# Two encoder layers on one core: the second layer's rows 1024 to 1535 in halves, the order of the residual work, and a windowed rule for repeated score matmuls

## The chip, the cores and the metric

The kernel runs on one core of a Trainium2 chip (trn2). The metric is the device time of one execution in microseconds, the median of several runs. Only bf16 inputs and a bf16 output of 2048 x 512 cross the memory; everything else stays on the core.

## What is computed

Two identical layers, each an attention block with a residual, then a dense block with a residual:

```python
# x: 1 x 2048 x 512, H = 32 heads of Dh = 16, Dff = 1792
def _A_ref(x, wqkv, wo):
    q, k, v = ...                       # (x @ wqkv) split into 3 x 32 heads of 16
    scores = jnp.einsum("bhqd,bhkd->bhqk", q, k) * (Dh ** -0.5)
    p = _softmax(scores, axis=-1)
    o = jnp.einsum("bhqk,bhkd->bhqd", p, v)
    return (o to B, S, D) @ wo

def _B_ref(x, w1, w2):
    h = jnp.maximum(x @ w1, 0)
    return h @ w2

x = x + _A_ref(_layernorm(x), A_wqkv, A_wo)
x = x + _B_ref(_layernorm(x), B_w1, B_w2)
x = x + _A_ref(_layernorm(x), A_wqkv, A_wo)
x = x + _B_ref(_layernorm(x), B_w1, B_w2)
```

Each layer has 32 x 2048 x 2048 exponentials, and both products around them have only 16 as one of their sizes.

## The kernel before

The program is one long unrolled stream, ordered by a list scheduler that runs while the program is built. It keeps a model of the time on TensorE (PE) and VectorE (DVE), in nanoseconds, and decides from it what is issued next.

The stream is cut into **slots**. A slot makes three blocks of scores (each 128 keys x 512 queries of one head, four heads side by side in the 32-row groups of the array), into three banks of PSUM; ScalarE (ACT) takes their exponential in one instruction. In some slots the third block goes to VectorE instead, which computes the exponential of two such blocks (a **pair**) with a polynomial in six kinds of step (`lin`, `step`, `cube`). PV products of earlier slots, and **residual work**, fill TensorE between the score triples. Residual work of a chunk of rows is: the output projection (o), the second layernorm with its transposes, the first dense product with relu (h), the second dense product (z), and in layer one also the next layernorm, k and v. It waits in the queue `work`.

The rows of a layer are worked through in chunks; `TPC` is 4 tiles of 128 rows. Layer two's last 512 rows are already cut in two:

```python
    chunks = {(l, j): (j * TPC, TPC) for l in range(2) for j in range(NQS)}   # NQS = 4
    chunks[1, NQS - 1] = (NKB - TPC, TPC // 2)
    chunks[1, NQS] = (NKB - TPC // 2, TPC // 2)
```

When the last head of a chunk has ended, its residual work goes behind all that still waits:

```python
    def before(l, j):          # whose buffers this chunk overwrites
        if (l, j) == (0, 0):
            return None
        return (l, min(j, NQS - 1) - 1) if j else (0, NQS - 1)

    def rest_of_chunk(l, j):
        b = before(l, j)
        xj, a, w = columns(l, j)
        n = w // P
        war_h = each(chunks[b][1], "z", *b) if b else []
        war_x = each(NF, "h", *b) if b else []
        gs = [o_group(l, j, i) for i in range(n)]
        gs += ln_groups(("ln2", l, j), xn2T, a, n, war_x)
        gs += [h_group(l, j, ft, war_h) for ft in range(0, NF, QS // w)]
        if (l, j) != (1, NQS - 1):
            gs += [z_group(l, j, i) for i in range(n)]
        ...                                        # layer one: ln1, k, v of the next layer
        return gs
    ...
        if ended[l, j] == NT and not last:
            work.extend(rest_of_chunk(l, j))
```

How much residual work a slot gets is paced so that it ends about with the next chunk, and it is only issued where the model leaves room before the next scores are needed:

```python
        pace = ( ... max(todo / max(rest + (0.0 if first["j"] == NQS - 1 and not first["l"] else AHEAD[first["l"]] if first["j"] < NQS - 1 else -6.0), 6.0), 0.5) )
        owed[0] = min(owed[0] + pace, 6.0) if todo else 0.0
        ...
        need_by = exp_end[no - 1] - MM - PE_TO_ACT
        limit = max(need_by - 60.0, s_ready) - SWITCH
```

A slot may write its three score blocks more than once, with the same values, to keep TensorE streaming; how often is found from the work of this slot alone and a small carry `level`:

```python
        spare = int(max(need_by - pe_start("s", s_ready), 0.0) / MM)       # MM = 216
        soon = (len(pend) > 1) + (owed[0] > 1.0 and (bool(cur) or not evac))
        short = FLOOR * 1330.0 - level - busy[0] - MM * (1 + soon)         # FLOOR = 0.56
        times = 1 + min(spare, max(0, math.ceil(short / MM)))
        ...
        for _ in range(times):
            pe_run("s", 1, s_ready)
            for a, (sg, kb, g) in sorted(zip(place, now), key=in_turn):
                nc.tensor.matmul(b[:, a : a + sg["w"]], kt[...], qbuf[...], start=True, stop=True,
                                 tile_position=(32 * g, 0))
        ...
        ex = nc.scalar.activation(out=eb[:, 0 : place[m]], in_=b[:, 0 : place[m]], func=ACTF.Exp, ...)   # L1249
```

After the last slot comes a tail that is written out by hand: what is left in the queue (`run_all`), then o, layernorm, h and z of the last 256 rows, and between them the z of the 256 rows before, whose two tiles of 128 rows are `half_part(0, ...)` (during the layernorm) and `half_part(1, ...)` (one matmul after each step of h):

```python
    run_all()
    l, j = 1, NQS
    ...                                     # o of the last rows, x, layernorm
    half_part(0, range(NF))
    ...                                     # transposes
    for ft in range(NF + 1):
        if ft < NF:
            ...                             # 4 matmuls of h (256 wide), relu on ACT or DVE in turn, load of w1
        if ft:
            for i in rows:
                add(banks[i], ht[ft - 1][:, part(i)], w2[:, ft - 1, :], False, ft == NF, "h")
        if ft < NF:
            half_part(1, [ft])
```

Of the kernel before, what the change touches and what calls it, by code (L numbers as in the profile page):

```python
# [24 lines left out]
def kernel(  # L25
# [20 lines left out]
    NF = DFF // P  # L46
    NTT = S // P
    NKB = S // P
    NDC = D // P
    QS = 512  # L50
    NQS = S // QS
    TPC = QS // P
# [20 lines left out]
    MM = 216.0  # L73
# [7 lines left out]
    AHEAD = (8.0, 8.0)  # L81
# [8 lines left out]
    LATE = 0.0  # L90
    BACKLOG = 6000.0
    HASTE = 12
    FULL = 3

    ctx.enter_context(tc.manual_schedule())
# [129 lines left out]

    slot = [0]
    now_pe = [0.0]
    now_dve = [0.0]  # L230
    mode = [None]
# [21 lines left out]
    def pe_start(kind, ready=0.0):  # L253
        return max(now_pe[0] + (SWITCH if mode[0] != kind else 0.0), ready)

    def pe_run(kind, units, ready=0.0):
        now_pe[0] = pe_start(kind, ready) + units * MM
        mode[0] = kind
        busy[0] += units * MM

# [7 lines left out]
    work = []  # L268
# [169 lines left out]


    chunks = {(l, j): (j * TPC, TPC) for l in range(2) for j in range(NQS)}  # L440
    chunks[1, NQS - 1] = (NKB - TPC, TPC // 2)
    chunks[1, NQS] = (NKB - TPC // 2, TPC // 2)

    def columns(l, j):

# [72 lines left out]
    def ln_rows(tag, tt, n, i):  # L518

        if tag not in ln_seq:  # L520
            ln_seq.append(tag)
        at_tag = ln_seq.index(tag)
        prev = ln_seq[at_tag - 1]
        old = [("xn", ln_seq[at_tag - 2], k) for k in range(TPC)] if at_tag > 1 else []
        if ("st", tag, i) not in made:
            task(830, lambda: ln_stats(tag, tt + i, i), [("st", tag, i)], old)
        if i == n - 1:

            def rstd():
                ln_rstd(tag, 0)  # L530
                ln_newton(tag)
                mark(("rs", tag, 3), lag=RSTD_LAG)

            task(500, rstd, [("rs", tag, 3)], each(n, "st", tag) + old)
            for k in range(n):
                task(
                    325, lambda k=k: ln_apply(tag, tt + k, k), [("xn", tag, k)],
                    [("xT", prev, k), ("rs", tag, 3)],
                )

    def ln_groups(tag, dst, at_column, n, war):
        groups = []
        for i in range(n):

            def piece(i=i):
                pt = ln_transpose(tag, i)

                def fin():
                    a = at_column + i * P
                    nc.vector.tensor_copy(out=dst[:, :, a : a + P], in_=pt)  # L550
                    mark(("xnT", tag, i))

                put_evac(342, fin)

            groups.append(
                group([(1.3, piece)], [("xT", tag, i), ("xnT", tag, i)], [("xn", tag, i)] + war)
            )
        return groups

    def each(n, *key):  # L560
        return [key + (i,) for i in range(n)]
# [63 lines left out]
    def o_group(l, j, i):  # L625
        tt, n = chunks[l, j]
        a = columns(l, j)[1] + i * P

        def fin(b):
            nc.vector.tensor_add(out=x_t[tt + i][:], in0=x_t[tt + i][:], in1=b)  # L630
            mark(("o", l, j, i))
            ln_rows(("ln2", l, j), tt, n, i)

        return mm_group(
            [(ot[t][:, a : a + P], wo[:, t // 2, :]) for t in range(NT)], fin,
            [("o", l, j, i)],
            [("ot", l, j, t, i) for t in range(NT)],
        )
# [11 lines left out]
    def h_group(l, j, ft, war):  # L650
        n = (l * NQS + j) * NF + ft
        _, a, w = columns(l, j)

        number = QS // w
        fts = range(ft, ft + number)
        made_here = [("h", l, j, f) for f in fts]

        def fin(b):
            out = htp[ft // 2][:, ft % 2 : ft % 2 + number, a : a + w]
            sums = b.rearrange("p (f q) -> p f q", f=number)  # L660
            if ending[0]:
                nc.scalar.activation(out=out, in_=sums, func=ACTF.Relu)
            else:
                nc.vector.tensor_scalar(  # L664
                    out=out, in0=sums, scalar1=0.0, scalar2=None, op0=ALU.max
                )
            for key in made_here:
                mark(key)

        def after():  # L670
            for f in range(number):
                load_w1(n + f + NW1)

        return mm_group(
            [
                (w1buf[(n + f) % NW1][:, c, :], xn2T[:, c, a : a + w])
                for f in range(number) for c in range(NDC)
            ],
            fin, made_here,
            each(w // P, "xnT", ("ln2", l, j)) + war + [("w1", n + f) for f in range(number)],  # L680
            after=after, wide_by=w, sums=number,
        )
# [20 lines left out]
    def before(l, j):  # L703

        if (l, j) == (0, 0):
            return None
        return (l, min(j, NQS - 1) - 1) if j else (0, NQS - 1)

    def rest_of_chunk(l, j):

        b = before(l, j)
        xj, a, w = columns(l, j)
        n = w // P
        war_h = each(chunks[b][1], "z", *b) if b else []
        war_x = each(NF, "h", *b) if b else []
        gs = [o_group(l, j, i) for i in range(n)]
        gs += ln_groups(("ln2", l, j), xn2T, a, n, war_x)
        gs += [h_group(l, j, ft, war_h) for ft in range(0, NF, QS // w)]
        if (l, j) != (1, NQS - 1):
            gs += [z_group(l, j, i) for i in range(n)]  # L720
        if l == 0:
            gs += ln_groups(("ln1", 1, j), xnT[j], 0, TPC, [])
            gs.append(k_group(1, 0, j))
            gs += [v_group(1, kb) for kb in range(j * TPC, (j + 1) * TPC)]
            gs += [k_group(1, T, j) for T in range(1, 4)]
        return gs
# [20 lines left out]
    for l in range(2):  # L747


        if l == 0:  # L750
            steps = [(0, range(4), 0, TPC), (0, range(MID), TPC, 2 * TPC)]
            steps += [(0, range(MID), 2 * TPC, NKB), (0, range(MID, 4), TPC, NKB)]
            steps += [(j, range(4), 0, NKB) for j in range(1, NQS)]
        else:
            steps = [(0, range(4), 0, NKB - TPC), (1, range(NEXT), 0, NKB - TPC)]
            steps += [(0, range(4), NKB - TPC, NKB), (1, range(NEXT, 4), 0, NKB)]
            steps += [(1, range(NEXT), NKB - TPC, NKB)]
            steps += [(j, range(4), 0, NKB) for j in range(2, NQS + 1)]
        for j, Ts, a, b in steps:
            for T in Ts:  # L760
                sums = acc[8 * j :] if l else acc0
                add_run(l, j, T, range(a, b), load=a and sums, store=b < NKB and sums)
# [7 lines left out]
    def finish_segment(sg, last):  # L770
# [93 lines left out]
            cost = 105 + 1.1 * width + (200 + 1.05 * width if quick else 0)  # L864
            task(cost, spread_mul, ots + [("m", n)], [("r", n)] + war)
        if ended[l, j] == NT and not last:
            work.extend(rest_of_chunk(l, j))

    pend = deque()
    musts = []  # L870
# [269 lines left out]
    while units:  # L1140
# [67 lines left out]
        if first["l"] and first["early"]:  # L1208
            rest = sum(x[0][0]["early"] for x in itertools.islice(units, 400)) / W - 20.0
        pace = (  # L1210
            3.0 if first["short"] and not first["l"] else max(todo / max(rest + (0.0 if first["j"] == NQS - 1 and not first["l"] else AHEAD[first["l"]] if first["j"] < NQS - 1 else -6.0), 6.0), 0.5)
        )
        owed[0] = min(owed[0] + pace, 6.0) if todo else 0.0
        hurry[0] = pace > (
# [14 lines left out]
        soon = (len(pend) > 1) + (owed[0] > 1.0 and (bool(cur) or not evac))  # L1229
        short = FLOOR * 1330.0 - level - busy[0] - MM * (1 + soon)  # L1230
        times = 1 + min(spare, max(0, math.ceil(short / MM)))
        b = ps_s[no % 2][:].rearrange("p w q -> p (w q)")
        eb = ebuf[no % NE]
        place = [sum(x[0]["w"] for x in now[:n]) for n in range(len(now) + 1)]
# [47 lines left out]
    run_all()  # L1282
    ending[0], wide[0] = False, True
    users.clear()
    l, j = 1, NQS
    tag = ("ln2", l, j)
    tt, n_rows = chunks[l, j]
    rows = range(n_rows)
# [58 lines left out]
    for ft in range(NF + 1):  # L1347
        if ft < NF:
            n = (l * NQS + j) * NF + ft
            b = more[ft % 4]  # L1350
            for c in range(NDC):
                add(
                    b, w1buf[n % NW1][:, c, :], xn2T[:, c, at_column : at_column + width],
                    c == 0, c == NDC - 1, "xnT",
                )
            if ft % 2:
                out = nc.scalar.activation(out=ht[ft][:, at_column : at_column + width], in_=at_bank(b)[:, 0:width], func=ACTF.Relu)
            else:
                out = nc.vector.tensor_scalar(
                    out=ht[ft][:, at_column : at_column + width], in0=at_bank(b)[:, 0:width],  # L1360
                    scalar1=0.0, scalar2=None, op0=ALU.max,
                )
            uses(out, b, "h")
            load_w1(n + NW1)
        if ft:
            for i in rows:
                add(
                    banks[i], ht[ft - 1][:, part(i)], w2[:, ft - 1, :],
                    False, ft == NF, "h",
                )  # L1370
        if ft < NF:
            half_part(1, [ft])
    for i in rows:
        copy = nc.vector.tensor_copy if i % 2 else nc.scalar.copy
        uses(copy(out=x_t[tt + i][:], in_=at_bank(banks[i])), banks[i])
# [33 lines left out]
```

The softmax here doesn't subtract the row's maximum and nothing guards it: scores larger than these inputs give would overflow.

## Time and profile before

| | |
|---|---|
| time, median of 3 runs | 1649.41 us (1643.58 to 1651.98) |
| profiled execution | 1656.09 us, span 1654.3 us |
| granted TensorE clock over the span | 0.981 |
| exponentials on ACT, 1536 columns / 1024 columns | 749 / 616 |
| polynomial pairs on DVE | 308 |
| score matmuls, 512 columns / 256 columns | 4396 / 1164 |
| last exponential ends | 1606.06 us |

The page gives each engine's busy share over the whole span; since the stages differ, the shares say less than the waits. In a line of groups, the first figures after the bar are busy time in us and the mean duration of one in ns, and after the second bar stands how long the engine had stood idle before them, with what ended that wait. Neighbouring instructions of an engine may overlap by part of their length, so a mean duration can exceed the distance between two starts. In a table of windows every line is a stretch of the span, with each engine's busy time in it and the granted share of TensorE's clock.

### The profile page before, as it was taken

Reading aid. Unit: us, or ns where it says so; the run is one execution under the profiler, and the core shown is the slowest. Engines: PE = TensorE matmul, PEld = TensorE weight load, DVE = VectorE, ACT = ScalarE, POOL = GpSimd, SP = SyncE. Lnnn points to the kernel's source line nnn. Section 1 sums busy time; section 2 is a strip of 40 time slices with the busy share of each in tenths; the row PEclk is TensorE's granted clock in tenths of the full one; section 3 lists DMA queues with packets and bytes.
Section 4 is the critical chain, followed back from the end, with each engine's and each line's share of the span. In section 5 each row is a group of like instructions: output and inputs, shape, how many; then the busy total and the mean of one; then the engine's idle time right before and its main releaser. Section 6 shows DMA issues by size and latency. Waiting matters only on the chain.

```text
span 1654.3 us, 32685 instructions
## 1 busy us (share of the span) xinstructions
PE 1509.3 (91%) x13512; PEld 493.4 (30%) x13512; DVE 1507.4 (91%) x3102; ACT 1590.0 (96%) x1393; POOL 86.7 (5%) x260
## 2 busy tenths in 40 slices
PE   8998889999989999999999998899999899999987
PEld 3222222222222222222222222223222222333334
DVE  7359999999999999899899998799999999999992
ACT  7999999999999999899999999999999999999982
POOL 2000001001010010100100000001000100010010
PEclk9999999999999999799999999899999999989999
DMA  5000000110002000021000100001200021001103
GB/s 160 1 1 2 2 2 15 40 27 15 2 17 47 20 13 8 11 46 24 9 1 17 30 1 1 2 3 23 45 16 21 13 48 27 16 18 35 33 16 89
DMA packets 104260, 37.92 MB, mean 23 GB/s; under 512 B 93712, under 2 KB 101648, under 8 KB 104112
## 3 DMA queue, kind: packets, MB, share of 16 engines
q1 hardware_dynamic: 92192, 24.38, 6.4%
q0 software_dynamic: 10576, 10.16, 3.2%
q8 instruction: 105, 1.72, 0.4%
q10 hardware_dynamic: 1344, 1.31, 0.2%
q14 instruction: 43, 0.35, 0.1%
HBM read 22.54 MB, written 2.10 MB: 15 GB/s over the span
## 4 chain that ended last, share of the span: by engine, by line
ACT 83%; PE 10%; DVE 5%; issue 1%; DMA 0%; POOL 0%; POOLq 0%; ACTq 0%; DVEq 0%
ACT e L1249 83%; PE ps_s L1240 3%; PE ps_o L876 3%; PE ps_f L430 2%; DVE lin L970 1%; PE ps_s L1303 1%; DVE stats L459 0%; DVE step L1010 0%; PE ps_f L510 0%; DVE cube L1018 0%; DMA w<-in_B_w_dram 0%; PE ps_s L430 0%; DVE cube L1019 0%; DVE cube L1022 0%; PE ps_f L1303 0%
## 5 line engine op out<-in xcount | busy, mean ns | idle before, releaser
L1249 ACT ACTIVATE e<-ps_s 128x1536 bf16<-128x1536 f32 (+1 forms) x1366 | 1575.4, 1400 | 14.5 <-PE ps_s L1240 13.9
L1240 PE MATMUL ps_s<-q,ktp 32*128 32x512 bf16 (+1 forms) x5560 | 610.6, 365 | 102.3 <-ACT e L1249 87.5
L876 PE MATMUL ps_o<-e,vaug 128*32 128x512 bf16 (+1 forms) x3906 | 523.5, 370 | 9.0 <-DVE u L800 3.1
L970 DVE TENSOR_SCALAR lin<-ps_s 128x512 int16<-128x512 f32 x616 | 419.8, 684 | 29.0 <-PE ps_s L1240 24.3
L1240 PEld LDWEIGHTS <-ktp 32*128 32x128 bf16 x5560 | 185.7, 92 | 527.5 <-issue 402.3
L876 PEld LDWEIGHTS <-vaug 128*32 128x32 bf16 x6012 | 157.8, 94 | 358.5 <-issue 346.3
L1010 DVE TENSOR_SCALAR step<-lin 128x1024 int16<-128x1024 int16 x616 | 242.5, 417 | 0.4
L1018 DVE TENSOR_TENSOR cube<-step 128x1024 f16<-128x1024 bf16 x308 | 209.2, 681 | 1.8 <-PE ps_o L876 0.2
L1022 DVE TENSOR_TENSOR cube<-cube,lin 128x1024 bf16<-128x1024 f16 x308 | 208.5, 677 | 0.0
L876 PE MATMUL ps_o<-cube,vaug 128*32 128x512 bf16 (+1 forms) x702 | 150.5, 363 | 0.0
L876 PE MATMUL ps_o<-step,vaug 128*32 128x512 bf16 (+1 forms) x702 | 145.8, 363 | 0.0
L876 PE MATMUL ps_o<-lin,vaug 128*32 128x512 bf16 (+1 forms) x702 | 129.5, 361 | 6.0 <-DVE u L800 3.8
L1019 DVE TENSOR_SCALAR cube<-cube 128x1024 f16<-128x1024 f16 x308 | 127.4, 415 | 1.3
L430 PE MATMUL ps_f<-xn2T,w 128*128 128x512 bf16 (+1 forms) x408 | 122.8, 384 | 3.3 <-DVE ht L664 1.3
L430 PE MATMUL ps_f<-w,ht 128*128 128x512 bf16 x392 | 121.0, 384 | 1.2 <-DVE q L607 0.5
L827 POOL DMA_DIRECT2D r<-u x45 | 32.6, 725 | 1202.9 <-DVE lin L970 590.4
L430 PE MATMUL ps_f<-xnT,wqkv 128*128 128x512 bf16 (+1 forms) x312 | 91.2, 376 | 3.9 <-DVE x L690 0.9
L607 DVE TENSOR_SCALAR q<-ps_f,qmask 128x512 bf16<-128x512 f32 (+1 forms) x94 | 63.4, 697 | 14.2 <-PE ps_f L430 13.9
L430 PE MATMUL ps_f<-wo,ot 128*128 128x512 bf16 x240 | 73.9, 384 | 1.2 <-DVE x L630 0.8
L664 DVE TENSOR_SCALAR ht<-ps_f 128x512 bf16<-128x512 f32 x98 | 67.1, 684 | 1.4 <-PE ps_f L430 0.9
L459 DVE BATCH_NORM_STATS2 stats<-x 128x6 f32<-128x512 bf16 x64 | 43.7, 683 | 16.2 <-ACT x L1313 14.1
L430 PEld LDWEIGHTS <-w 128*128 128x128 bf16 x448 | 35.5, 100 | 66.0 <-issue 49.6
(93 smaller groups left out, 607.0 us busy)
## 6 DMA issues: line engine op xcount, KB each, us to landing
w<-in_B_w_dram SPq DMA_DIRECT2D x126, 128.0 KB
r<-u POOLq DMA_DIRECT2D x32, 256.0 KB, 7.1
out_dram<-x SPq DMA_DIRECT2D x16, 128.0 KB
x<-in_A_x_dram SPq DMA_DIRECT2D x14, 128.0 KB
w<-in_B_w_dram SPq DMA_DIRECT2D x1, 1792.0 KB
r<-u POOLq DMA_DIRECT2D x13, 128.0 KB, 4.5
wqkv<-in_A_wqkv_dram ACTq DMA_DIRECT2D x2, 512.0 KB
c<-u SPq DMA_DIRECT2D x56, 8.0 KB
```

Of the source, the lines that this page charges most:

```text
L430: nc.tensor.matmul(out, lhsT, rhs, start=i % k == 0, stop=i % k == k - 1)
L459: nc.vector.bn_stats(out=st[:], in_=x_t[tt][:])
L607: return nc.vector.tensor_scalar(out=qbuf[n % 2][e][:, 0:w], in0=b, scalar1=qmask[e][:, 0:1], scalar2=None, op0=ALU.mult,)
L664: nc.vector.tensor_scalar(out=out, in0=sums, scalar1=0.0, scalar2=None, op0=ALU.max)
L876: nc.tensor.matmul(ps_o[32 * g : 32 * g + 32, 0 : sg["w"]], vaug[sg["l"]][kb][:, 4 * sg["T"] + g, 2 * e : 2 * e + 32], rhs, start=g not in ...
L970: first = nc.vector.tensor_scalar(out=lin[which][:, half * QS : (half + 1) * QS], in0=src, scalar1=EXP_BIAS, scalar2=0.0, op0=ALU.add, op1 ...
L1010: nc.vector.tensor_scalar(out=stair, in0=line, scalar1=keep, scalar2=put, op0=ALU.bitwise_and, op1=ALU.bitwise_or,)
L1018: (609, lambda: nc.vector.tensor_mul(out=power, in0=mantissa, in1=mantissa)),
L1019: (342, lambda: nc.vector.tensor_scalar(out=power, in0=power, scalar1=CUBE, scalar2=None, op0=ALU.mult)),
L1022: (609, lambda: nc.vector.tensor_mul(out=power.bitcast(BF16), in0=power, in1=line.bitcast(BF16))),
L1240: nc.tensor.matmul(b[:, a : a + sg["w"]], kt[32 * g : 32 * g + 32, kc : kc + P], qbuf[sg["n"] % 2][sg["e"]][32 * g : 32 * g + 32, 0 : sg[" ...
L1249: ex = nc.scalar.activation(out=eb[:, 0 : place[m]], in_=b[:, 0 : place[m]], func=ACTF.Exp, scale=1.0 / (LOG2E * UNIT),)
```

## The change

Layer two's rows 1024 to 1535 become two chunks of 256 rows as well, so that layer two has chunks 0, 1 (512 rows) and 2 to 5 (256 rows). The output projection and second layernorm of a chunk that has just ended go ahead of all older residual work instead of behind it. One of the two z tiles that the tail computed (`half_part(1, ...)`) is put into the queue. And beside the rule per slot there is a second one for repeating the score triples: the model notes when it believes TensorE to stream, and a triple is repeated, within the same `spare`, until the last 3413 ns before its end hold at least 60% of streaming. The aim of the first three is to have residual work spread over the slots instead of left over at the end; that of the last is to keep the clock of TensorE from being lowered. The diff, with cuts:

```diff
+    WINDOW, BUSY, IDLE = 3413.0, 0.6, 0.6
...
+    ran = deque(maxlen=60)
+    def share(end, more=0.0):
+        done = sum(min(b, end) - max(a, end - WINDOW) for a, b in ran if b > end - WINDOW and a < end)
+        return (done + more) / WINDOW
+
     def pe_run(kind, units, ready=0.0):
         now_pe[0] = pe_start(kind, ready) + units * MM
+        ran.append((now_pe[0] - units * MM, now_pe[0]))
...
-    chunks[1, NQS - 1] = (NKB - TPC, TPC // 2)
-    chunks[1, NQS] = (NKB - TPC // 2, TPC // 2)
+    HALF = TPC // 2
+    for n in range(4):
+        chunks[1, 2 + n] = (2 * TPC + n * HALF, HALF)
+    LAST = 5
...
     def before(l, j):
-        return (l, min(j, NQS - 1) - 1) if j else (0, NQS - 1)
+        if not j:
+            return 0, NQS - 1
+        rows = chunks[l, j][0] % TPC
+        return max(
+            (l, b) for b in range(j)
+            if chunks[l, b][1] == TPC or chunks[l, b][0] % TPC == rows
+        )
...
     def rest_of_chunk(l, j):
-        gs = [o_group(l, j, i) for i in range(n)]
-        gs += ln_groups(("ln2", l, j), xn2T, a, n, war_x)
-        gs += [h_group(l, j, ft, war_h) for ft in range(0, NF, QS // w)]
-        if (l, j) != (1, NQS - 1):
-            gs += [z_group(l, j, i) for i in range(n)]
+        work[0:0] = [o_group(l, j, i) for i in range(n)] + ln_groups(
+            ("ln2", l, j), xn2T, a, n, war_x
+        )
+        gs = [h_group(l, j, ft, war_h) for ft in range(0, NF, QS // w)]
+        gs += [z_group(l, j, i) for i in range((l, j) == (1, LAST - 1), n)]
...
-            steps += [(j, range(4), 0, NKB) for j in range(2, NQS + 1)]
+            steps += [(j, range(4), 0, NKB) for j in range(2, LAST + 1)]
...
-        pace = (... AHEAD[first["l"]] if first["j"] < NQS - 1 else -6.0 ...)
+        pace = (... AHEAD[first["l"]] if first["j"] < (LAST if first["l"] else NQS - 1) else -6.0 ...)
...
         times = 1 + min(spare, max(0, math.ceil(short / MM)))
+        floor = BUSY if soon > 1 else IDLE
+        begin = pe_start("s", s_ready)
+        while times <= spare and share(begin + times * MM, times * MM) < floor:
+            times += 1
...
-    l, j = 1, NQS
+    l, j = 1, LAST
...
-        if ft < NF:
-            half_part(1, [ft])
```

More of the change, by code (lines that the diff above doesn't have):

```diff
@@ L224, in uses @@
         log.append((ins.ins, w, makes))
-    slot = [0]
     now_pe = [0.0]
@@ L523, in ln_rows @@
         prev = ln_seq[at_tag - 1]
-        old = [("xn", ln_seq[at_tag - 2], k) for k in range(TPC)] if at_tag > 1 else []
+        rows_of_prev = chunks[prev[1:]][1]
+        before_that = ln_seq[at_tag - 2] if at_tag > 1 else None
+        old = each(chunks[before_that[1:]][1], "xn", before_that) if at_tag > 1 else []
         if ("st", tag, i) not in made:
@@ L537, in ln_rows @@
                     325, lambda k=k: ln_apply(tag, tt + k, k), [("xn", tag, k)],
-                    [("xT", prev, k), ("rs", tag, 3)],
+                    [("xT", prev, k)] * (k < rows_of_prev) + [("rs", tag, 3)],
                 )
@@ L866, in finish_segment @@
         if ended[l, j] == NT and not last:
-            work.extend(rest_of_chunk(l, j))
+            later = rest_of_chunk(l, j)
+            work.extend(later)
     pend = deque()
@@ L1210 @@
         pace = (
-            3.0 if first["short"] and not first["l"] else max(todo / max(rest + (0.0 if first["j"] == NQS - 1 and not first["l"] else AHEAD[first["l"]] if first["j"] < NQS - 1 else -6.0), 6.0), 0.5)
+            3.0 if first["short"] and not first["l"] else max(todo / max(rest + (0.0 if first["j"] == NQS - 1 and not first["l"] else AHEAD[first["l"]] if first["j"] < (LAST if first["l"] else NQS - 1) else -6.0), 6.0), 0.5)
         )
```

## The prediction

> **What bounds the kernel now.** I read the page's busy shares and its chain first. They name ScalarE.
>
> ```profile
> PE 1509.3 (91%) x13512; PEld 493.4 (30%) x13512; DVE 1507.4 (91%) x3102; ACT 1590.0 (96%) x1393; POOL 86.7 (5%) x260
> ...
> ACT 83%; PE 10%; DVE 5%; issue 1%; DMA 0%; POOL 0%; POOLq 0%; ACTq 0%; DVEq 0%
> ...
> L1249 ACT ACTIVATE e<-ps_s 128x1536 bf16<-128x1536 f32 (+1 forms) x1366 | 1575.4, 1400 | 14.5 <-PE ps_s L1240 13.9
> ```
>
> Of the chain that ended last, 83% is one line, the exponential. It ran 1575.4 us in 1366 slots and stood idle only 14.5 us before its instances, 13.9 us of it for scores. So between the first and the last slot only two things can move the time: fewer columns on ScalarE (more blocks for the polynomial on VectorE), or less of those 13.9 us. All else is in the tail, after the last slot.
>
> Next I looked for where the 13.9 us lie. Most slices of the page show the full clock; I laid windows of 3.41 us against the two longest dips. Columns: window, its length, busy us (instructions) of PE, PEld, DVE, ACT and POOL, granted clock, DMA share, GB/s.
>
> ```profile
> 675.11:678.53 3.42, 3.08 (x28) 0.91 (x27) 3.35 (x8) 3.42 (x3) 0.28 (x1) 1.00 0.21 36
> 678.53:681.94 3.41, 1.93 (x19) 0.61 (x18) 3.34 (x11) 3.41 (x5) 1.11 (x5) 1.00 0.19 41
> 681.94:685.35 3.41, 3.41 (x26) 0.68 (x22) 2.80 (x6) 2.70 (x4) 2.58 (x8) 0.50 0.03 7
> 685.35:688.77 3.42, 3.42 (x25) 0.92 (x25) 2.06 (x7) 3.30 (x3) 0.00 (x0) 0.50 0.00 0
> 688.77:692.18 3.41, 3.41 (x24) 0.82 (x20) 2.62 (x7) 1.81 (x2) 0.00 (x0) 0.50 0.00 0
> ```
> ```profile
> 1460.16:1463.57 3.41, 1.88 (x38) 1.09 (x39) 3.34 (x10) 3.41 (x4) 2.10 (x8) 1.00 0.02 1
> 1463.57:1466.99 3.42, 3.42 (x52) 1.41 (x46) 2.39 (x6) 2.85 (x3) 1.77 (x6) 0.50 0.04 6
> ```
> What ran in the first of these trigger windows, at 678.53:
> ```profile
> L1240 PE MATMUL ps_s<-q,ktp 32*128 32x512 bf16 x12 | 1.4, 378 | 1.6 <-ACT e L1249 1.6
> L876 PE MATMUL ps_o<-e,vaug 128*32 128x512 bf16 x7 | 0.8, 390 | 0.0
> ```
>
> The reader is to see the sequence: one window in which PE has little to do, then half clock for several windows, in which ScalarE waits. Twelve score matmuls are four triples of 0.216 us each, and seven PV matmuls in four column groups are about two more units (216 ns is the spacing of full-width matmuls in the tail of this trace): 6 x 0.216 = 1.3 us, 38% of the window. In both windows POOL is busy: it is iterating the second layernorm, there is no residual matmul to run, and PE waits for ScalarE. Three shorter dips at 64, 1057 and 1074 us follow windows with PE busy 2.25, 2.13 and 2.10 of 3.41 us. The ScalarE time missing in the stretches of half clock and the window after them is 0.7 + 4.7 + 3.2 + 0.9 + 3.2 = 12.7 us, so nearly all of the 13.9.
>
> Last, the end, in stages around the last slot at 1606.06:
> ```profile
> 1414.00:1510.00 96.00, 89.48 (x1309) 36.85 (x1310) 90.16 (x196) 92.85 (x82) 8.20 (x19) 0.93 0.11 22
> 1510.00:1606.06 96.06, 89.93 (x1335) 35.42 (x1333) 93.48 (x200) 96.06 (x85) 5.65 (x10) 1.00 0.13 27
> 1606.06:1623.50 17.44, 12.05 (x78) 6.72 (x76) 5.21 (x12) 3.58 (x6) 1.96 (x9) 0.80 0.40 90
> 1623.50:1654.30 30.80, 23.99 (x142) 13.23 (x141) 8.43 (x27) 6.61 (x14) 0.00 (x0) 1.00 0.28 69
> ```
> The tail is 48.2 us. Its first 17.4 us are not work of the last 256 rows at all, but the layernorm and the first dense product of the 256 rows before them:
> ```profile
> 1613.27 1.91 PE L430 MATMUL ps_f<-xn2T,w 128*128 128x256 bf16 x8
> 1613.51 0.60 ACT L662 ACTIVATE ht<-ps_s 128x512 bf16<-128x512 f32 x1 [7.45 <-PE ps_s L430]
> ```
> They are there because the queue is first in, first out: by the output-projection matmuls in the trace, rows 1024-1535 begin their residual work at about 1425 us and rows 1536-1791 only at about 1594 us, although their attention ended near 1510.
>
> [...]
>
> **The change, part by part.**
>
> *Residual work first, with halves.* A full chunk of 512 rows has 32 units of o, about 5 of transposes, 56 of h and 56 of z, some 150 units of 0.216 us. A half has 75. From the end of rows 512-1023 (about 1224 us, when some 40 units of older work are left) to the last slot are some 341 slots. The new order asks in them for 40 + 150 + 75 + 75 + 61 (the last but one half without one z) + 32 for q = 433 units, 1.27 a slot. The trace shows 1.1 to 1.2 units a slot in h stretches (22 matmuls in 1490-1510, about 18 slots) and 1.5 to 1.6 in z stretches (31 in 1550-1570). With this mixture I get about 1.25 to 1.35: it just fits. So the 17.4 us of h leave the tail.
>
> *The new tail.* After the last slot T: PV 0.8 us, copy 0.4, shuffle 0.44, reciprocal 0.95, multiply 0.35, last o matmul and cast 1.0, together 3.9, then the second row's reciprocal, multiply, matmul and cast behind them, some 1.6: T + 5.5 us. The layernorm, 4.4 us as now (1629.1 to 1633.5), with one z row still beneath it. From there to the end is 20.8 us now. The ft loop now has a period of 1.085 us: four half-width matmuls (0.435) and three full ones (0.65). One full one goes: 0.87. The w1 loads came every 0.88 us in the h stretch at 1615-1623, so I take 0.88: 14 x 0.2 = 2.9 us less. T + 5.5 + 4.4 + 17.9 = T + 27.8 against T + 48.2: **20 us less**.
>
> *Cost of the halves on VectorE.* From the groups by shape, two halves against one whole: q 2 x 476 - 743 = 209 ns, copy of sums 2 x 418 - 680 = 156, multiply 209, reciprocal 2 x 192 - 241 = 143: 717 ns in each of 8 heads' segments, 5.7 us. What comes forward from the tail: seven evictions of h at 0.684, two rows of layernorm and copies 1.6, one z 0.7: 7.1 us. With 0.5 for one more rsqrt start: 13.3 us on an engine that is 97% busy in the last 96 us. A pair of polynomial blocks costs 2 x 684 + 2 x 417 + 681 + 677 + 415 = 3975 ns there, and saves ScalarE 2 x (1593 - 1166) = 854 ns. 13.3 / 3.98 = 3.3 pairs lost: **+2.9 us**. Half-width scores don't slow the slots: 85 slots in the undisturbed 96.06 us are 1.13 us each, as elsewhere (134 in 150 us at 530-680).
>
> *Repeated triples.* They take only time that the builder's model holds to be spare before the scores are needed, so ScalarE should not see them. Two more in a window of 38% make it 51%. With leftover work now behind o and the layernorm, the lulls at 678 and 1460 are also filled. I count on two thirds of 12.7 us: **-8.5 us**. The median run may have had less to lose than the profiled one, which took 1656.09.
>
> *Sum*: 1649.4 - 20.4 + 2.9 - 8.5 = 1623.4; I add 1.6 for a busier PE and predict **1625**.
>
> **Rivals.** (1) *PE takes the bound.* More residual work and more triples in the same slots: the scores come late, ScalarE waits, or h is still left over at the end. For it: PE is busy 93% in the last two stages and the fit above is tight. Against it: at 1510-1606 ScalarE was busy for all 96.06 us at the highest residual rate seen. It would give back 5 to 12 us: 1630 to 1637. (2) *The clock dips stay*, since the builder's timeline is not the chip's: the present rule with FLOOR already aims at 0.56 and still let 0.38 through[...]. Then only the tail counts: about 1632. (3) *All dips vanish*, with the VectorE time lost in them: 13.9 us and some three pairs (2.6 us) more: about 1617. (4) *Loads hide the tail's gain*: w1 arriving every 0.88 us makes the loop no faster if the loads start late; then +3 us.
>
> **Range and chances.** The tail's 20 us hardly depend on the rest, so slower than before needs rivals 1 and 2 and something unseen. The three runs before span 8.4 us, so a median can be off by some 4 us. I take 1612 to 1640. Faster by over 2% means under about 1616.4, near rival 3 plus a better tail: 0.22. Within 2%: 0.76. Slower: 0.02.
>
> **What would show it.** Right: L662 on ScalarE gone from the tail, last slot to end about 28 us; no half clock at the layernorms of layer two's last chunks; wait of line e for scores under 6 us; pairs (308 now) a few fewer; more score matmuls than 4396 and 1164. Wrong: xn2T matmuls of the main loop still after the last slot (rival 1), a wait for scores spread over slots at full clock (rival 1), as much half clock as now (rival 2). The prediction fails altogether if pairs drop by twenty or more, for then VectorE's load, which I put at 13 us, was mis-sized.

## The result and the profile after

The changed kernel takes **1630.37 us** (median of 4 runs, 1629.62 to 1630.93) against 1650.54 us before (4 runs): a ratio of 0.9886, 95% interval 0.9857 to 0.9915. So it is 1.1% faster, 20 us, within the range and 5 us above the prediction. That the sum came out near does not mean that its terms did: the runs below show that one part of the change brought more than its share and another cost time.

The page of the kernel after, busy shares, chain and costliest group:

```profile
PE 1467.9 (90%) x14783; PEld 516.2 (32%) x14974; DVE 1513.4 (93%) x3146; ACT 1584.2 (97%) x1386; POOL 95.4 (6%) x279
...
ACT 81%; DVE 8%; PE 7%; issue 3%; DMA 1%; POOL 0%; ACTq 0%; DVEq 0%
...
L1272 ACT ACTIVATE e<-ps_s 128x1536 bf16<-128x1536 f32 (+1 forms) x1366 | 1573.6, 1402 | 7.0 <-PE ps_s L1263 5.7
```

ScalarE is still the bound, with the same 1366 slots and 1573.6 us of exponentials (1575.4 before). Its idle time before them is halved, from 14.5 to 7.0 us. The two dips of the clock that the prediction showed are gone. One stretch of half clock remains, 10.24 us long; these are windows of a third of that length, 3.41 us, around it (window, length, busy us and instructions of PE, PEld, DVE, ACT, POOL, granted clock, DMA share, GB/s):

```profile
182.35:185.76 3.41, 1.96 (x25) 0.61 (x22) 3.27 (x7) 3.41 (x4) 0.00 (x0) 1.00 0.00 0
185.76:189.18 3.42, 3.42 (x25) 0.83 (x28) 2.88 (x7) 2.55 (x3) 0.00 (x0) 0.50 0.00 0
...
192.59:196.00 3.41, 2.94 (x12) 0.63 (x13) 1.80 (x5) 1.98 (x2) 0.00 (x0) 0.50 0.00 0
```

It looks as before: one window with PE busy 1.96 of 3.41 us, then a granted clock of 0.50, in which ScalarE is busy for only 2.55 and 1.98 us of the windows shown. The new rule did not prevent it.

The end, in stages around the last slot, which now ends at 1596.96 us:

```profile
1500.00:1596.96 96.96, 88.89 (x1422) 41.86 (x1430) 94.59 (x205) 96.96 (x85) 7.58 (x18) 1.00 0.20 43
1596.96:1605.46 8.50, 8.23 (x49) 4.07 (x49) 4.04 (x9) 0.60 (x2) 0.00 (x0) 1.00 0.29 69
1605.46:1629.10 23.64, 17.35 (x108) 9.96 (x110) 8.50 (x28) 5.58 (x12) 0.00 (x0) 1.00 0.30 73
```

The tail, from the last slot to the end, is 32.2 us instead of 48.2. Between the two profiled executions lie 25.2 us: 16.1 in the tail and 9.1 before the last slot. What delays the first cast of the tail (1605.46) is seen in the timeline of this stretch (start, duration, what, and the idle time before it with what ended it):

```profile
1597.69 1.05 PE L438 MATMUL ps_f<-xn2T,w 128*128 128x256 bf16 x8
1597.79 0.42 DVE L818 COPY u<-ps_o 128x256 f32<-128x256 f32 x1 [0.71 <-PE ps_o L895]
...
1598.79 2.97 PE L438 MATMUL ps_s<-w,ht 128*128 128x512 bf16 x13
...
1602.48 0.43 DVE L855 STREAM_SHUFFLE r<-u 128x256 f32<-128x256 f32 x1
```

One group of h (8 matmuls of half width, 4 units of a full matmul's 0.216 us) and the z tile that the change had put into the queue (14 matmuls; one record is missing) were still waiting when the last slot ended: 18 units. They run first, and the last head's shuffle comes 4.7 us after its sums were copied.

### The profile page after: what moved, and what is told of

It reads as the page before. It is cut to its first block, busy times and chain, and to the rows that moved or that the text cites. A ratio compares the mean times of both kernels' runs of the same rounds, so it can differ in the third digit from the quotient of the medians.

```text
span 1629.1 us, 35605 instructions
## 1 busy us (share of the span) xinstructions
PE 1467.9 (90%) x14783; PEld 516.2 (32%) x14974; DVE 1513.4 (93%) x3146; ACT 1584.2 (97%) x1386; POOL 95.4 (6%) x279
## 4 chain that ended last, share of the span: by engine, by line
ACT 81%; DVE 8%; PE 7%; issue 3%; DMA 1%; POOL 0%; ACTq 0%; DVEq 0%
ACT e L1272 81%; DVE lin L989 2%; PE ps_s L1263 2%; PE ps_f L438 2%; PE ps_o L895 1%; DVE cube L1037 1%; DVE step L1029 1%; PE ps_s L1326 1%; DVE cube L1041 1%; DVE ot L831 0%; DVE stats L469 0%; DVE ht L676 0%; DVE cube L1038 0%; DVE x L702 0%; DMA u<-c 0%
## 5 line engine op out<-in xcount | busy, mean ns | idle before, releaser
L1272 ACT ACTIVATE e<-ps_s 128x1536 bf16<-128x1536 f32 (+1 forms) x1366 | 1573.6, 1402 | 7.0 <-PE ps_s L1263 5.7
L895 PE MATMUL ps_o<-e,vaug 128*32 128x512 bf16 (+1 forms) x4340 | 517.5, 345 | 13.3 <-DVE u L818 6.2
L1263 PEld LDWEIGHTS <-ktp 32*128 32x128 bf16 x6283 | 195.2, 91 | 502.0 <-issue 365.9
L895 PEld LDWEIGHTS <-vaug 128*32 128x32 bf16 x6680 | 169.3, 94 | 349.1 <-issue 337.3
L895 PE MATMUL ps_o<-cube,vaug 128*32 128x512 bf16 (+1 forms) x780 | 143.6, 340 | 0.7 <-issue 0.5
L895 PE MATMUL ps_o<-lin,vaug 128*32 128x512 bf16 (+1 forms) x780 | 123.6, 338 | 7.0 <-DVE u L818 5.0
L438 PE MATMUL ps_f<-w,ht 128*128 128x512 bf16 x336 | 104.5, 383 | 5.8 <-issue 4.1
L845 POOL DMA_DIRECT2D r<-u x52 | 37.8, 726 | 1166.5 <-DVE lin L989 545.2
L438 PE MATMUL ps_f<-xnT,wqkv 128*128 128x512 bf16 (+1 forms) x287 | 83.8, 362 | 8.0 <-issue 2.4
L438 PE MATMUL ps_f<-wo,ot 128*128 128x512 bf16 x209 | 64.6, 383 | 3.9 <-issue 2.9
L831 DVE SCALAR_TENSOR_TENSOR ot<-u,mask,r 128x512 bf16<-128x512 f32 (+2 forms) x82 | 51.4, 628 | 1.1
```

The lines of the kernel that those rows point to most:

```text
L438: nc.tensor.matmul(out, lhsT, rhs, start=i % k == 0, stop=i % k == k - 1)
L831: nc.vector.scalar_tensor_tensor(out=ot[t][:, at_column + a : at_column + a + w], in0=u[:, a : a + w], scalar=mask[e][:, 0:1], in1=r[:, a ...
L895: nc.tensor.matmul(ps_o[32 * g : 32 * g + 32, 0 : sg["w"]], vaug[sg["l"]][kb][:, 4 * sg["T"] + g, 2 * e : 2 * e + 32], rhs, start=g not in ...
L1263: nc.tensor.matmul(b[:, a : a + sg["w"]], kt[32 * g : 32 * g + 32, kc : kc + P], qbuf[sg["n"] % 2][sg["e"]][32 * g : 32 * g + 32, 0 : sg[" ...
```

## The experiments

All runs are of variants of the kernel after, unless they say otherwise. The clock was granted at 0.50 in every lowered stretch of the traces before and after, so the time of half clock is worked out as 2 x (1 - granted clock) x span of the profiled execution; the clock has three digits, so it is good to about 2 us. Repeated triples are the score matmuls above those of the kernel that repeats none (3072 of full and 2048 of half width; 3584 and 1024 where rows 1024-1535 are whole), divided by 3 and 6.

| kernel | triples repeated | ScalarE idle before exponentials | half clock | last slot ends | tail | median, ratio to before [95% interval] |
|---|---|---|---|---|---|---|
| before | 294 | 14.5 | 63 | 1606.1 | 48.2 | 1650.5 |
| after | 342 | 7.0 | 10 | 1597.0 | 32.2 | 1630.4, 0.9886 [0.9857, 0.9915] |
| rule alone | 383 | 18.0 | 20 | 1612.7 | 45.8 | 1664.1, 1.0070 [1.0050, 1.0090] |
| no rule | 278 | 3.4 | 0 | 1593.8 | 27.9 | 1624.7, 0.9836 [0.9821, 0.9850] |
| work in turn | 395 | 29.8 | 23 | 1625.2 | 42.2 | 1672.3, 1.0123 [1.0087, 1.0159] |
| whole chunk | 363 | 8.1 | 3 | 1595.9 | 35.8 | 1637.0, 0.9907 [0.9888, 0.9927] |
| order alone | 292 | 2.8 | 3 | 1591.0 | 32.7 | 1627.9, 0.9860 [0.9827, 0.9893] |
| halves alone | 301 | 17.4 | 33 | 1610.0 | 39.1 | 1652.3, 1.0003 [0.9983, 1.0023] |
| floor 0.7 | 582 | 14.8 | 3 | 1608.7 | 40.2 | 1655.4, 1.0020 [1.0005, 1.0034] |
| no repeats | 0 | 22.5 | 135 | 1617.0 | 30.3 | 1651.7, 1.0008 [0.9987, 1.0029] |
| whole, no rule | 292 | 3.6 | 7 | 1592.0 | 34.5 | 1628.6, 0.9856 [0.9829, 0.9884] |
| rule when empty | 288 | 4.5 | 13 | 1595.8 | 29.1 | 1625.8, 0.9849 [0.9807, 0.9890] |
| steps first | 342 | 5.1 | 3 | 1594.5 | 32.3 | 1630.3, 0.9865 [0.9836, 0.9894] |
| after again | 342 | 6.7 | 16 | 1598.3 | 32.2 | 1632.5, 0.9882 [0.9852, 0.9912] |

Medians of one line are of one chip; the ratio is what compares across lines. Idle, half clock, last slot and tail are of one profiled execution each, in us. Half clock above all varies between the executions of one kernel: the 20 executions of halves alone were granted 0.973 to 0.995 of the clock.

### The rule alone, and everything but the rule

My theory at first was that of the prediction: two separate gains, a shorter tail by order and halves, and the clock kept by the rule and by leftover work. To the kernel before, the rule alone (the lines for `WINDOW`, `ran` and `share`, as in the change, left out):

```diff
...
+        floor = BUSY if soon > 1 else IDLE
+        begin = pe_start("s", s_ready)
+        while times <= spare and share(begin + times * MM, times * MM) < floor:
+            times += 1
```

> The kernel before with the windowed rule for repeated triples and nothing else. Theory A (the gain is two separate things, a shorter tail from the order and halves of the residual work, and clock kept by the rule and by leftover work): the tail after the last exponential stays at 48 us, the stretches of half clock shrink from 61 us to under 30, ScalarE's wait for scores from 14 to 5-9 us; time 1638-1646. Rival B (the rule is most of the gain): under 1636. Rival C (the rule does nothing, leftover work filled the lulls): 1648-1652 with the same half clock as before.

And the kernel after without it:

```diff
-    WINDOW, BUSY, IDLE = 3413.0, 0.6, 0.6
+    WINDOW, BUSY, IDLE = 3413.0, 0.0, 0.0
```

> The changed kernel with the windowed rule switched off (both floors 0), so only halves, order and the moved z tile. Theory A: tail about 32 us as with the change, but some half clock comes back (10-40 us of it), ScalarE waits 8-12 us for scores; time 1632-1640. Rival B: 1640 or more. Rival C: 1629-1631 with one or no dip.

All the theories fail here. The rule alone made the kernel before **slower**, by 0.7%. It did raise the clock, as meant: in its profiled execution a third of the half clock is left, and its four executions were granted 0.988 to 0.994 against a median of 0.985 before. But ScalarE stood idle 18.0 us instead of 14.5, and four pairs fewer went to VectorE (304), so that its exponentials took 1578.6 us instead of 1575.4. ScalarE's wait for scores (us in total, times, longest), and what TensorE waited for at the end of the longest (4.7 us, up to 828.25):

```profile
ACT e L1262 <- PE ps_s L1253: 15.2, 24, 4.7
```
```profile
827.60 0.61 PE L1253 MATMUL ps_s<-q,ktp 32*128 32x512 bf16 x2 [0.25 <-DVE ktp L576]
```

There the last part of k (`ktp`) of layer two was made at the moment in which its scores needed it. By the copies out of `ps_f`, the kernel with the rule had finished 167 groups of residual work at slot 600, the kernel before 172.

And without the rule the changed kernel is faster than with it, and its profiled execution has no half clock at all (granted clock 1.000). The clock in the slices of its page (9 is 90% or more), and ScalarE's wait:

```profile
PEclk9999999999999999999999999999999999999999
```
```profile
ACT e L1272 <- PE ps_s L1263: 3.2, 6, 1.1
```

Its tail is free of leftovers, as these two stages show (last slot to first cast of the tail, and from there to the end):

```profile
1593.82:1598.19 4.37, 4.16 (x24) 1.91 (x25) 3.38 (x7) 0.00 (x1) 0.00 (x0) 1.00 0.00 0
1598.19:1621.70 23.51, 17.14 (x108) 9.83 (x108) 8.43 (x27) 5.52 (x12) 0.00 (x0) 1.00 0.30 74
```

The second stage is equal to the one with the rule (23.64); the first is 4.37 against 8.50 us. What the rule costs in the tail is just that difference.

The clock does not explain the difference. The four executions without the rule were granted 1.000, 0.998, 0.998 and 0.996, the four with it 0.997, 0.997, 0.998 and 0.998. At 0.998, which both have, they took 1624.69 and 1624.70 us against 1629.62 and 1629.82: 5 us for the rule at the same clock (the kernel before took 1651.8 and 1650.5 us beside them).

### The order undone, and the halves undone

```diff
-        work[0:0] = [o_group(l, j, i) for i in range(n)] + ln_groups(
-            ("ln2", l, j), xn2T, a, n, war_x
-        )
-        gs = [h_group(l, j, ft, war_h) for ft in range(0, NF, QS // w)]
+        gs = [o_group(l, j, i) for i in range(n)]
+        gs += ln_groups(("ln2", l, j), xn2T, a, n, war_x)
+        gs += [h_group(l, j, ft, war_h) for ft in range(0, NF, QS // w)]
```

> The changed kernel with the output projection and layernorm of a chunk behind the older residual work again; halves and rule kept. Theory A (total residual work against room on TensorE decides what is left at the end; the order only fills the lulls at the layernorms): the tail is 32-38 us, the rule keeps most of the clock, 1631-1637. Rival D (the order is what empties the tail): h of rows 1536-1791 is in the tail again, tail over 42 us, 1640 or more.

```diff
-    for n in range(4):
-        chunks[1, 2 + n] = (2 * TPC + n * HALF, HALF)
-    LAST = 5
+    for n in range(2):
+        chunks[1, 3 + n] = (3 * TPC + n * HALF, HALF)
+    LAST = 4
```

> The changed kernel with rows 1024-1535 as one chunk of 512 again; order, rule and moved z tile kept. Theory A: the 150 units of that chunk arrive at once with 171 slots to go and 61 more behind them, 1.3 to 1.4 units a slot with q, more than TensorE has room for: 20-40 units left over, the tail 36-41 us, 1634-1640. Rival D (order alone empties the tail): 1628-1632. Rival E (halves are the whole of the tail's gain): tail 46-48 us, 1643 or more.

The order was worth far more than I had thought: without it, and with the rule, the kernel is slower than before, and h is in the tail again (rival D). The idle time of ScalarE of 29.8 us has one large piece, seen in the timelines of TensorE and ScalarE (for the kernel with work in turn):

```profile
1278.72 1.89 PE L438 MATMUL ps_f<-wo,ot 128*128 128x512 bf16 x8 [0.80 <-DVE x L702]
1281.39 1.89 PE L438 MATMUL ps_f<-wo,ot 128*128 128x512 bf16 x8 [0.78 <-DVE x L642]
1284.05 1.89 PE L438 MATMUL ps_f<-wo,ot 128*128 128x512 bf16 x8 [0.78 <-DVE x L642]
1286.72 1.89 PE L438 MATMUL ps_f<-wo,ot 128*128 128x512 bf16 x8 [0.78 <-DVE x L642]
```
```profile
1288.98 2.36 ACT L1271 ACTIVATE e<-ps_s 128x1536 bf16<-128x1536 f32 x2 [10.60 <-PE ps_s L1262]
```

By the program's order these are the four o groups of rows 512-1023, which had stood in the queue until a head of the next chunk needed the buffer `ot` that they read. The builder then had to issue all four at once, one after another through the single bank `ps_f`, each waiting for VectorE's addition, and no scores in between: 10.60 us. The whole chunk with rule and order is at 1637.0, within theory A's range, but see below for what of it is the rule's.

### Order alone, halves alone, and the number of repeats

From here on my theory (A2 in the expectations) is that the order brings the gain and repeats take room that residual work needs. To the kernel before, the order alone:

```diff
-        gs = [o_group(l, j, i) for i in range(n)]
-        gs += ln_groups(("ln2", l, j), xn2T, a, n, war_x)
-        gs += [h_group(l, j, ft, war_h) for ft in range(0, NF, QS // w)]
+        work[0:0] = [o_group(l, j, i) for i in range(n)] + ln_groups(
+            ("ln2", l, j), xn2T, a, n, war_x
+        )
+        gs = [h_group(l, j, ft, war_h) for ft in range(0, NF, QS // w)]
```

> The kernel before with the output projection and layernorm of an ended chunk ahead of older residual work, and nothing else. Theory A2 (formed after the first four runs: leftover work behind the layernorm fills its lull and so keeps the clock; halves let the end be clear of leftovers; the rule's repeats take room from residual work and cost time): half clock falls from 61 us to under 25, last exponential at 1590-1600, tail 38-46 because rows 1024-1535 still come at once; 1632-1644. Rival F (halves keep the clock too): half clock as before, 1645-1652.

This one move gives 1627.9 us, ratio 0.9860, as much as the whole change (0.9886; the intervals overlap). ScalarE's line shows what became of the 14.5 us:

```profile
L1251 ACT ACTIVATE e<-ps_s 128x1024 bf16<-128x1024 f32 (+1 forms) x1366 | 1571.9, 1407 | 2.8 <-PE ps_s L1242 2.1
```

It has no more repeats than the kernel before (292 triples against 294). In the profiled execution it kept the clock in all slots (0.999 was granted over the span and 0.97 in the tail; 0.996 to 0.999 over the span in its four executions), and its tail is 32.7 us, shorter than I expected of it; 14 matmuls of `half_part(1, ...)` are still in that tail. The layernorm of rows 1024-1535 of layer one, which in the kernel before ran at 680.50 us into an empty queue, now comes at 654.55. First the groups on TensorE while GpSimd iterates in the kernel with the order alone (654.55 to 659.90 us), then the same in the kernel before (680.50 to 685.10 us, mostly at half clock):

```profile
L878 PE MATMUL ps_o<-e,vaug 128*32 128x512 bf16 x15 | 2.4, 390 | 0.0
L1242 PE MATMUL ps_s<-q,ktp 32*128 32x512 bf16 x15 | 1.8, 381 | 0.7 <-ACT e L1251 0.6
L430 PE MATMUL ps_f<-xnT,wqkv 128*128 128x512 bf16 x4 | 1.4, 387 | 0.0
```
```profile
L1240 PE MATMUL ps_s<-q,ktp 32*128 32x512 bf16 x21 | 3.1, 548 | 1.0 <-ACT e L1249 1.0
L876 PE MATMUL ps_o<-e,vaug 128*32 128x512 bf16 x8 | 1.6, 499 | 0.0
L876 PE MATMUL ps_o<-step,vaug 128*32 128x512 bf16 x2 | 1.2, 608 | 0.0
```

The lull is now filled by k of the next layer (`xnT,wqkv`, copied to `ktp` in this stretch), which is older work that waits behind, and by more of PV (15 matmuls in 5.35 us against 8 in 4.60 on line e). In the kernel before there was no residual matmul at all in this lull; the clock fell at 681.94, after the window with four triples that the prediction shows. With the order alone the windows stay at full clock:

```profile
654.41:657.82 3.41, 3.33 (x30) 0.99 (x29) 3.36 (x7) 3.41 (x4) 2.77 (x7) 1.00 0.00 0
657.82:661.23 3.41, 2.78 (x27) 0.99 (x25) 3.29 (x8) 3.41 (x4) 1.64 (x6) 1.00 0.00 0
```

Halves alone are the kernel after with the floors at 0 and the work in turn (both edits above).

> The changed kernel without the windowed rule and with residual work in turn again: halves and the moved z tile are left. Theory A2: dips at the layernorms as before in layer one (the one near 682), a forced finish of o near 1290 is possible but shorter than the 10.6 us with the rule; tail 28-34 us; 1632-1645. Rival F: under 1630, no half clock.

Nothing is gained (1652.3 us, ratio 1.0003, above the range expected): the dips are back, 33 us of half clock, and so is a forced finish of o, for which ScalarE waits 6.8 us, up to 1270.64. The tail is 39.1 us, between the 48.2 before and the 32.2 after, longer than expected.

More repeats, by the floor:

```diff
-    WINDOW, BUSY, IDLE = 3413.0, 0.6, 0.6
+    WINDOW, BUSY, IDLE = 3413.0, 0.7, 0.7
```

> The changed kernel with the rule's floor at 0.7 instead of 0.6: more repeats. Theory A2 (a repeat takes room from residual work): 80 or more triples more than with 0.6, more left over after the last exponential (tail 36-48 us against 32), more forced waits of ScalarE; 1640-1665. Rival G (repeats are free, and what differs between 0 and 0.6 was chance of the schedule): 1626-1634 with a tail near 28-34 and the half clock gone.

And none at all (floors 0 and the old rule off):

```diff
-    FLOOR = 0.56
+    FLOOR = 0.0
```

> The changed kernel with no repeated triple at all (both rules off). If the old rule's repeats too only take room: 1620-1625, no half clock, tail 28. If they hold the clock: windows of low streaming appear, 40-150 us of half clock, 1635-1665. Theory A2 holds the second more likely[...].

Both came as theory A2 had it. With 278, 342 and 582 repeated triples the tail is 27.9, 32.2 and 40.2 us and the time 1624.7, 1630.4 and 1655.4 us. With none the tail does not shrink further (30.3; eight matmuls of the last z tile are left over), and the clock goes: 135 us of half clock, as the page of that kernel shows in its slices,

```profile
PEclk9999679999999999999899999879999999999999
...
L1263 PE MATMUL ps_s<-q,ktp 32*128 32x512 bf16 (+1 forms) x5120 | 556.3, 350 | 133.7 <-ACT e L1272 112.2
```

and the gain of the order and halves is lost entirely. So repeats do hold the clock here: 0.947 to 0.959 of it was granted in the twelve executions without any, 0.996 to 1.000 in the four of the kernel with the old rule alone. The old rule already made enough of them, and the new one added 64 that cost more than they kept.

### What the rule's repeats displace, and what halves are worth beside the order

```diff
-        while times <= spare and share(begin + times * MM, times * MM) < floor:
+        while not todo and times <= spare and share(begin + times * MM, times * MM) < floor:
```

> The changed kernel with the windowed rule allowed only in slots in which no residual work waits at all. Theory A3 (the rule costs because its repeats take the place of residual work that could have run a little later): the cost goes, tail 28-30 us, 1623-1627. Rival H (the repeats cost in some other way, by late scores or a chance of the schedule): 1629-1634 as with the rule.

With the rule allowed only where no residual work waits, 54 of its 64 triples vanish and so does its cost: tail 29.1 us, 1625.8 us. Nearly all its repeats were thus made while work waited that the model did not yet let in. The intervals overlap, 0.9849 [0.9807, 0.9890] against 0.9882 [0.9852, 0.9912] on the same chip, but at the same granted clock the two stay apart: 1626.66 against 1632.71 us at 0.996, and 1624.61 and 1625.02 against 1631.12 at 0.997.

This run alone does not show that the repeats cost *because* work waited, since hardly any others were left to compare. The traces show where the work stayed behind: by the copies out of `ps_f`, the changed kernel had finished 366 groups of residual work at slot 1300 and 378 at slot 1350, without the rule 368 and 384. In these fifty slots it repeated ten triples, without the rule three. Its other extra repeats, 51 of them before slot 1000, had left it only two groups behind.

Whole, without the rule:

```diff
-    for n in range(4):
-        chunks[1, 2 + n] = (2 * TPC + n * HALF, HALF)
-    LAST = 5
+    for n in range(2):
+        chunks[1, 3 + n] = (3 * TPC + n * HALF, HALF)
+    LAST = 4
-    WINDOW, BUSY, IDLE = 3413.0, 0.6, 0.6
+    WINDOW, BUSY, IDLE = 3413.0, 0.0, 0.0
```

> The changed kernel with rows 1024-1535 whole and the windowed rule off: order and moved z tile are left. If the halves are worth little beside the order (theory A3: the order is the gain, the rule a cost): tail 28-32 us, no half clock, 1622-1628, as without the rule and with halves (1624.7). If the halves are needed to be clear at the end: tail 34 or more, 1630 or more.

1628.6 us, a little above the range of the first expectation, and a tail of 34.5 us, as in the second: neither fits whole. Against the halves without the rule the tail is 6.6 us longer and the last slot 1.8 us earlier; it has 309 pairs against 306. By the medians the halves are worth 4 us (and 4 at the same clock of 0.998: 1628.26 and 1628.88 against 1624.7, on another chip), but the two intervals of the ratios overlap, so their worth beside the order is likely and not settled.

The fourth part of the change, the z tile moved into the queue, can be read off here too: up to the last slot this kernel and the one with the order alone run the same 3080 VectorE instructions in the same order, so that they differ in the tail alone. Times are 1628.6 and 1627.9 us, tails 34.5 and 32.7. Without the halves the moved tile gains nothing; it is left over and runs in the tail.

Last, VectorE's part of the longer tail with the rule:

```diff
     ending[0] = True
+    for i in range(chunks[1, LAST][1]):
+        last_steps[0](i)
     run_all()
...
     for i in rows:
-        last_steps[0](i)
         add(banks[i], ot[NT - 1][:, part(i)], wo[:, (NT - 1) // 2, :], False, True)
```

> The changed kernel with the last head's shuffle, reciprocals and multiplications issued on VectorE ahead of the work left in the queue. If the 4.3 us by which the tail is longer than without the rule are VectorE waiting for the leftover z tile (copy at 1597.79, shuffle only at 1602.48): tail 28.5-30.5 us, 1626.5-1629. If TensorE's own leftover is what counts: tail 31.5-32.5, 1629.5-1631.

> The changed kernel itself, for comparison on this chip. 1629.5-1631.5, tail 32 us, one stretch of half clock or two.

The first theory of the run with the steps first is refuted. The shuffle did move up, and nothing followed from it. The timeline of the tail with the steps first:

```profile
1595.78 0.44 DVE L855 STREAM_SHUFFLE r<-u 128x256 f32<-128x256 f32 x1
...
1596.31 2.97 PE L438 MATMUL ps_s<-w,ht 128*128 128x512 bf16 x13
...
1599.33 1.67 PE L1328 MATMUL ps_s<-wo,ot 128*128 128x512 bf16 x7
```

TensorE works through the leftover h and z and only then takes up the last rows' o; 32.3 us as before the edit. It is TensorE's leftover that counts, 18 units of 0.216 us = 3.9 us of the 4.3. The changed kernel itself gave 0.9882 on that chip, as at first, though its 1632.5 us, at granted clocks of 0.993 to 0.997, lie above the 1629.5-1631.5 I had set.

## Why the prediction was right, and where its terms were not

**The bound and the two places to look** were right: the slots and their columns did not change (1366, 1573.6 us), and nearly all of the gain is in ScalarE's waits for scores and in the tail.

**The tail.** I predicted T + 27.8. Measured: 32.2 with the rule, 27.9 without it. Where nothing is left over the working holds part by part: from the last slot (1593.82) to the end of the second cast 5.4 us (5.5 predicted), the layernorm 4.4 (4.4), the rest 18.0 (17.9). The steps of the ft loop start 0.87 us apart (1614.49, 1615.36, 1616.23 in the kernel after), with TensorE not idle between them, but for one wait of 0.34 us for a load of w1 (1621.94). The unit of 0.216 us held too: 14 matmuls in an unbroken run of the tail (3.19 us from 1598.44 without the rule, from 1606.04 with it) start 216 ns apart. What failed is the step "433 units ... it just fits": with the rule's repeats it did not, by 18 units. Rival 1 named this ("h is still left over at the end"), and put it at 5 to 12 us; it was 4.3 in the tail.

**Order and halves in the tail.** The prediction named the right cause, "the queue is first in, first out", but priced order and halves together, and my first theory in the runs then put the tail's h down to a full chunk arriving at once. The order alone takes this h out of the tail all but for two groups, with the chunk whole; halves alone left a tail of 39.1 us. So it is the order that moved it, and the halves, beside the order, account for 6.6 us of tail.

**Cost of halves on VectorE.** 3.3 pairs lost, +2.9 us. Without the rule 306 pairs with halves and 309 without: three, as predicted. With the rule it was one (308 and 309), so the size is right only to about two pairs.

**Repeated triples, -8.5 us.** A repeated triple takes one unit in the trace: in the kernel before one triple takes 0.39 us at 92.32, and it and its repeat together 0.61. ScalarE's idle time fell by 7.5 us, so the size was nearly right. But the term named two causes, the repeats and the leftover work that now fills the lulls, and only the second is seen: the order alone brings the idle time from 14.5 to 2.8 us without more repeats. The step that failed is "They take only time that the builder's model holds to be spare before the scores are needed, so ScalarE should not see them". With the rule alone ScalarE stood idle 3.5 us longer, and in the changed kernel the rule left 18 units of work for the tail. Spare time in one slot is room in which residual work could have moved forward a slot later; filled with repeats, it is gone. The rule's term was not part of -8.5 but about **+5.7 us** (1624.7 to 1630.4; the intervals of the two ratios, 0.9821 to 0.9850 and 0.9857 to 0.9915, do not overlap), of which 4.3 lie in the tail.

**The sum.** -20.4, +2.9, -8.5, +1.6 were meant to give -24.4. Between the profiles it was -16.1 in the tail and -9.1 in the slots, -25.2; between the medians -20.2, since the profiled execution before was a long one. That the sum is near is partly luck: two errors in opposite directions are in it, an order that did more for the clock than I gave it, and a rule whose cost I took for a gain. The 1625 us predicted are the time of the kernel without the rule.

The dip at 186 us is not to be laid to the rule. Between the two profiles, with and without it, the slots are 0.2 us apart at slot 100, 4.2 at slot 150, just after the dip, and 3.1 at the last; but the clock lost changes between executions of the same program (granted 0.997 and 0.998 at first, 0.993 to 0.997 in the four of after again), and one execution without the rule lost as much (0.996). What stays open is why the same program loses more in one execution than in another, and whether each repeat displaces one group, which no run isolates.

## What to carry to other kernels

When a serial step (here a layernorm on small vectors) leaves an engine empty, put what leads to it ahead of the older work, so that the older work is still there to fill the gap; here this needed no new instruction and brought, by itself, as much as the whole change. Filler that is meant to be free must be tried with the rest of the queue: "spare" within one scheduling step may be what the next one lives on. And undo each part of a bundle by itself: here the bundle without one of its four parts is the best version measured, 1624.7 us, ratio 0.9836 [0.9821, 0.9850].

## What the hardware showed that I had not expected

In the kernel before TensorE is busy 91% of the span by the page, and still the clock was at 0.50 for 61 us of 1654; without any repeated triples it was so for 135 us of 1647. The windows ahead of the dips shown here were not idle: TensorE was busy for 1.93, 1.88 and 1.96 of 3.41 us in them. A window with 2.78 us, in the kernel with the order alone, was followed by full clock. In the traces before and after, the lowered stretches within the span are 6.83, 17.07, 10.24, 6.83, 13.65 and 6.83 us long, and 10.24 us, each a multiple of 3.41 us. I divided both traces, from 40 to 1560 us, into windows of 3.41 us in phase with these stretches. Of the windows at full clock, 4 have PE busy up to 2.00 us, and 3 of them were followed by half clock; the fourth, with 1.79 us (1199.54 us of the kernel after), was not. Of the 10 windows with 2.01 to 2.40 us, 3 were followed by half clock; of the 854 above that, none. In each dip shown, TensorE was busy throughout the first window of half clock (3.41 or 3.42 us), and the next window was at half clock too.
